# Normalised attention and a leaky-ReLU MLP on one core: the order of products in a half-Strassen batch, a softmax reciprocal one group later, and one multiply moved behind a maximum

## The chip, the core and the metric

The kernel runs on one core of a Trainium2 chip. The metric is the device time in microseconds of one execution. The core has engines that run side by side (in the kernel before, PE was busy for 96% of the span, ACT for 72% and DVE for 67%): TensorE for matmuls (PE in the profile, with PEld for its weight loads), VectorE (DVE), ScalarE (ACT), GpSimd (POOL) and SyncE (SP), which only issues transfers here. The profile lists the instructions of each, and beside a wait the instruction of another engine that ended it. The kernel puts its matmul results into banks of PSUM, and some matmuls have to wait until ACT or DVE has emptied a bank (0.42 us at 355.63, behind ACT's L575; 0.30 us by starts at 361.94, where DVE's L578 ran from 361.26 to 361.88). Idle time of PE in front of a matmul is called a stop here.

The kernel before took 424.06 us in the median of three runs (423.5 to 425.12), and 424.0 us in the median of six once the changed kernel was measured beside it.

## The reference

```python
q, k, v: (8, 12, 448, 64); w_in: (768, 2048); w_out: (2048, 768)
q_n, k_n = rmsnorm(q, g_q), rmsnorm(k, g_k)
scores = q_n @ k_n.T / 8
attn = exp(scores - max); attn = attn / (sum(attn) + 1e-9)
x = (attn @ v) as rows of 768
h = x @ w_in
out = maximum(0.01 * h, h) @ w_out
```

## The kernel before

The attention is cut into 24 units of four heads, three units to a batch. Each unit goes through four groups of score matmuls (L195), one step in the first and two in each other group. Between them PE works off a queue of MLP matmuls of an earlier batch, to keep PE busy. Batches 6 and 7 do part or all of the first MLP product by Strassen's scheme, which makes a product of 2 by 2 blocks from seven block products instead of eight. Batch 6 is the half-Strassen batch: eight plain row blocks ("M", six 448-column matmuls each, L363), and 14 products `(n, s)` of six 224-column matmuls (L565).

The code that the change touches, with cuts marked:

```python
def shift_max(u):                       # the first maximum of a unit, L232, and dg, L234 (DVE)
    ...
def shift_mm(u):                        # L244: dg spread by PE; L245: second maximum; L253: eb (DVE)
    ...
def ex(u):                              # L214: et = exp(scores + eb) (ACT); empties the score slot
    ...
def pv_out(u):                          # L295: P*V copied from PSUM to x32, a single buffer (ACT)
    ...
def zcol_inv(u):                        # L305, L306: 1/sum as Ln and Exp (ACT), then four DMAs to rz
    ...
def xmul_pool(u, eng=nc.gpsimd):        # L321: xt = x32 * rz; on DVE for units 4 to 6
    ...

LATE_HALF = ("M", "M", "M", "M", "M", (1, 2), (2, 2), (7, 2), "M", (6, 2), (1, 3), "M",
             (5, 2), (4, 2), (7, 3), (3, 2), (2, 3), (6, 3), "M", (5, 3), (4, 3), (3, 3))

for u in range(3, NU):                  # NU = 24
    for d in range(4):
        qk(u, STEPS[d])                 # L195
        if d == 0:
            shift_max(u)
            # ... pv_slot(u - 1); zcol(u - 1)
            shift_mm(u)
            pv_out(u - 1)
            zcol_sum(u - 1)
        ex(u)
        # ...
        if d == 0:
            job(zcol_inv, u - 1)
        if d == 1 and narrow(u - 1) and not 5 <= u < 8:
            xmul_pool(u - 1)
        # ... at d == 2: job(prep_rinv, u + 2), then two jobs prep_norm (L167, DVE)
        if d == 2 and 5 <= u < 8:
            job(xmul_sb, u - 1)         # the multiply on DVE
        fill(u, d, jobs)                # queue items, with jobs between them
```

The products of batch 6 share four PSUM banks. A product that starts a new sum needs a bank that an L357 (an M's leaky ReLU), an L575 (a product's leaky ReLU, both ACT) or an L578 or L584 (sums and copies on DVE) has emptied. Of these waits the profile lists 0.30 us for an L357 at 351.00 and 0.42 for an L575 at 355.63.

## Time and profile before

| what | value |
|---|---|
| median of three runs | 424.06 us |
| span of the profiled run | 421.4 us |
| PE busy | 403.2 us, 96% |
| ACT, DVE, POOL busy | 304.5, 282.1, 83.3 us |
| PE busy in 80-100 us | 18.81 of 20 us |
| PE busy in 350-370 us | 18.52 of 20 us |

PE is the engine that sets the time, and its work is the same in both kernels. The table is therefore read for where PE is not busy. The prediction below shows the lines of these places.

### The profile page before, as it was taken

Reading aid. Unit: us, or ns where it says so; the run is one execution under the profiler, and the core shown is the slowest. Engines: PE = TensorE matmul, PEld = TensorE weight load, DVE = VectorE, ACT = ScalarE, POOL = GpSimd, SP = SyncE. Lnnn points to the kernel's source line nnn. Section 1 sums busy time; section 2 is a strip of 40 time slices with the busy share of each in tenths; the row PEclk is TensorE's granted clock in tenths of the full one; section 3 lists DMA queues with packets and bytes.
Section 4 is the critical chain, followed back from the end, with each engine's and each line's share of the span. In section 5 each row is a group of like instructions: output and inputs, shape, how many; then the busy total and the mean of one; then the engine's idle time right before and its main releaser. Section 6 shows DMA issues by size and latency. Waiting matters only on the chain.

```text
span 421.4 us, 9149 instructions
## 1 busy us (share of the span) xinstructions
PE 403.2 (96%) x3731; PEld 217.4 (52%) x3731; DVE 282.1 (67%) x459; ACT 304.5 (72%) x474; POOL 83.3 (20%) x75
## 2 busy tenths in 40 slices
PE   8787999989999999999999999999999999999995
PEld 7454454444445544454445544454445556558953
DVE  5888675888569736576459736467349788547762
ACT  5999877768887689877987689867986666653600
POOL 1967432200010121210220120220110101010000
PEclk9999999999999999999999999999999999999999
DMA  8999996889664995678664796677542470212023
GB/s 273 230 251 258 237 252 91 210 154 199 163 152 75 213 242 98 160 175 176 156 144 78 214 192 139 169 151 186 156 88 45 120 162 2 45 39 75 2 53 98
DMA packets 71949, 62.39 MB, mean 148 GB/s; under 512 B 36324, under 2 KB 67044, under 8 KB 71908
## 3 DMA queue, kind: packets, MB, share of 16 engines
q1 hardware_dynamic: 61312, 49.62, 46.4%
q0 software_dynamic: 10272, 11.80, 18.0%
q8 instruction: 29, 0.48, 0.4%
q10 hardware_dynamic: 324, 0.39, 0.3%
q14 instruction: 12, 0.10, 0.1%
HBM read 45.61 MB, written 11.01 MB: 134 GB/s over the span
## 4 chain that ended last, share of the span: by engine, by line
PE 79%; DVE 9%; ACT 9%; issue 1%; DVEq 0%; ACTq 0%
PE hps L363 25%; PE sT L195 7%; PE sT L341 6%; ACT et L214 5%; PE ma L445 5%; PE md L445 5%; PE mc L445 5%; PE bank L445 5%; PE zc L283 3%; PE op L404 3%; PE bank L565 3%; PE mb L445 3%; DVE n L167 2%; PE warm L743 2%; PE sT L445 2%
## 5 line engine op out<-in xcount | busy, mean ns | idle before, releaser
L214 ACT ACTIVATE et<-sT,eb 128x896 f16<-128x896 f32 x166 | 159.6, 1010 | 17.8 <-PE sT L195 16.1
L363 PE MATMUL hps<-xt,win 128*128 128x448 f16 x594 | 119.9, 353 | 0.4 <-DVE xt L350 0.2
L363 PEld LDWEIGHTS <-win 128*128 128x128 f16 x612 | 56.6, 98 | 59.1 <-issue 10.8
L321 POOL TENSOR_TENSOR xt<-x,rz 128x896 f16<-128x896 f32 x16 | 33.7, 2104 | 145.8 <-DMA rz<-zs 122.7
L167 DVE TENSOR_TENSOR n<-rq,rinv 128x896 f16<-128x896 f32 (+2 forms) x25 | 26.7, 1070 | 52.5 <-ACT rinv L161 49.7
L195 PE MATMUL sT<-qkT 64*64 64x448 f16 x664 | 52.2, 363 | 4.3 <-ACT et L214 3.2
L357 ACT ACTIVATE gt<-hps 128x448 f16<-128x448 f32 x99 | 51.9, 548 | 5.5 <-PE hps L363 5.3
L155 DVE TENSOR_REDUCE ssq<-sq 128x14 f32<-128x896 f32 (+2 forms) x49 | 50.3, 1057 | 0.7 <-ACT sq L144 0.7
L445 PEld LDWEIGHTS <-sa 128*128 128x128 f16 x352 | 32.8, 98 | 26.3 <-issue 6.1
L295 ACT COPY x<-sT 128x896 f32<-128x896 f32 x19 | 17.2, 907 | 37.1 <-DVE sT L245 37.1
L124 POOL DMA_DIRECT2D vt<-in_v_dram x24 | 18.2, 757 | 115.6 <-PE sT L341 108.1
L445 PEld LDWEIGHTS <-gt 128*128 128x128 f16 x264 | 25.2, 98 | 18.7 <-issue 2.1
L195 PEld LDWEIGHTS <-qkT 64*64 64x64 f16 x672 | 15.4, 104 | 37.6 <-issue 32.8
L341 PE MATMUL sT<-et,vt 64*64 64x448 f16 x532 | 28.5, 349 | 0.3
L404 PE MATMUL op<-wout,gt 128*128 128x384 f16 x160 | 28.4, 327 | 0.0
L232 DVE TENSOR_REDUCE sT<-sT 128x1 f32<-128x896 f32 x22 | 24.1, 1094 | 4.7 <-PE sT L195 4.5
L341 PEld LDWEIGHTS <-vt 64*64 64x64 f16 x672 | 20.7, 107 | 11.3 <-issue 1.7
L167 DVE TENSOR_TENSOR n<-rk,rinv 128x896 f16<-128x896 f32 (+2 forms) x26 | 26.1, 1010 | 0.0
L404 PEld LDWEIGHTS <-gt 128*128 128x128 f16 x192 | 17.6, 98 | 14.6 <-issue 3.1
L445 PE MATMUL ma<-wout,gt 128*128 128x384 f16 x128 | 23.5, 326 | 0.0
L426 DVE TENSOR_TENSOR sa<-gt 128x512 f16<-128x512 f16 (+1 forms) x15 | 8.1, 542 | 16.0 <-ACT gt L357 12.1
L144 ACT ACTIVATE sq<-rq 128x896 f32<-128x896 f32 (+2 forms) x18 | 16.3, 913 | 1.2 <-DMA rq<-in_q_dram 1.2
(136 smaller groups left out, 526.8 us busy)
## 6 DMA issues: line engine op xcount, KB each, us to landing
rq<-in_q_dram SPq DMA_DIRECT2D x24, 448.0 KB, 4.3
rk<-in_k_dram SPq DMA_DIRECT2D x24, 448.0 KB, 5.7
out_dram<-ost SPq DMA_DIRECT2D x52, 192.0 KB, 2.9
rz<-zs SPq DMA_DIRECT2D x76, 112.0 KB, 2.3
vt<-in_v_dram POOLq DMA_DIRECT2D x24, 224.0 KB, 5.5
win<-in_moe_w_in_dram POOLq DMA_DIRECT2D x8, 384.0 KB, 12.7
wout<-in_moe_w_out_dram POOLq DMA_DIRECT2D x2, 1536.0 KB, 27.1
out_dram<-ost SPq DMA_DIRECT2D x4, 96.0 KB, 2.1
```

The source lines that it names most:

```text
L124: nc.gpsimd.dma_start(vts[u % NV].rearrange("p a t d -> p a (t d)"), rows(v, u))
L155: nc.vector.tensor_reduce(buf(u, "ssq")[:, ti, :, c[0]:c[1]], buf(u, f"sq{ti}")[:, :, c[0]:c[1]], axis=AXL.X, op=ALU.add)
L167: nc.vector.tensor_tensor(buf(u, "n16")[:, ti, c[0]:c[1]].rearrange("p s a d -> p a s d"), src[:, :, c[0]:c[1]], buf(u, "rinv")[:, ti, :, ...
L195: nc.tensor.matmul(banks[a][64 * r:64 * r + 64, 0:S].rearrange("p (t x) -> p t x", t=NS), kT(u, r, a, t), qT(u, r, a), start=True, stop=True)
L214: nc.scalar.activation(s["et"][:, t], sT[:, :, 0:S], AF.Exp, bias=s["eb"], scale=1.0)
L232: nc.vector.tensor_reduce(s["spare"][:, 511:512], sT[:, :, 0:S], axis=AXL.XY, op=ALU.max)
L321: eng.tensor_tensor(xts[b][:, g], s["x32"], s["rz"], op=ALU.mult)
L341: nc.tensor.matmul(s["pv"][r][64 * a:64 * a + 64, 0:S], vts[u % NV][64 * r:64 * r + 64, a, t], s["et"][64 * r:64 * r + 64, t, a], start=(t ...
L357: nc.scalar.activation(dst, src, AF.Prelu, bias=0.0, scale=1.0, alpha=0.01)
L363: nc.tensor.matmul(hps[:, 0:S], win16[:, kt // 2, kt % 2, ts(ft, P)], xt[:, kt // 2, kt % 2], start=(kt == 0), stop=(kt == KT - 1))
L404: nc.tensor.matmul(op2[:, 0:HC], gt[:, ft, ds(col(t), P)], wout16[:, ft, ds(HC * half, HC)], start=(ft == 0), stop=(ft == FT - 1))
L445: nc.tensor.matmul(bank[:, 0:HC], a[:, f], b[:, f], start=(first and f == 0), stop=(f == HF - 1), skip_group_check=not first)
```

## The change

The intent is to move three things out of PE's way: the products of batch 6 that ask for a bank too soon, the two activations of unit 22's reciprocal that delay the leaky ReLU of the last product, and the multiply of unit 4 that delays the first maximum of unit 6.

```diff
-    LATE_HALF = ("M", "M", "M", "M", "M", (1, 2), (2, 2), (7, 2), "M", (6, 2), (1, 3), "M", (5, 2), (4, 2), (7, 3), (3, 2), (2, 3),
-                 (6, 3), "M", (5, 3), (4, 3), (3, 3))
+    LATE_HALF = ("M", "M", "M", "M", "M", "M", (1, 2), (7, 2), (2, 2), (6, 2), "M", (1, 3), (5, 2), (4, 2), (7, 3), (3, 2), (6, 3),
+                 (2, 3), (5, 3), (4, 3), "M", (3, 3))
@@ two weight sums hung on other products
-                after[7, 2] = [lambda: win_sum(1, 0, (raws, "rq", 3))]
-                after[6, 2] = [lambda: win_sum(2, 0, (raws, "rk", 3))]
+                after[6, 2] = [lambda: win_sum(1, 0, (raws, "rq", 3))]
+                after[1, 3] = [lambda: win_sum(2, 0, (raws, "rk", 3))]
@@ unit 4's multiply
                         shift_max(u)
+                        if u == 6:
+                            xmul_sb(u - 2)
...
-                if d == 2 and 5 <= u < 8:
+                if d == 2 and 6 <= u < 8:
                     job(xmul_sb, u - 1)
@@ the last reciprocal
-                        job(zcol_inv, u - 1)
+                        if u < NU - 1:
+                            job(zcol_inv, u - 1)
...
-                if d == 1 and narrow(u - 1) and not 5 <= u < 8:
+                if d == 1 and narrow(u - 1) and not 5 <= u < 8 and u < NU - 1:
                     xmul_pool(u - 1)
+                if u == NU - 1:
+                    if d == 1:
+                        job(zcol_inv, u - 1)
+                    if d == 2:
+                        xmul_pool(u - 1)
```

## The prediction

> **What bounds the kernel now.** I read the busy shares, the slices and the chain of waits first, then PE's own waits, then the timeline around each of them, and last the program order of both kernels on each engine.
>
> ```profile
> PE 403.2 (96%) x3731; PEld 217.4 (52%) x3731; DVE 282.1 (67%) x459; ACT 304.5 (72%) x474; POOL 83.3 (20%) x75
> PE   8787999989999999999999999999999999999995
> ```
>
> PE has work nearly all the time, and the change neither adds nor removes a matmul (7461 rows on PE's program in both). So the only thing to win is time in which PE stands still. PE's busy time by stretch shows where: about 10 us are lost in the first 60 us, which the change leaves alone; then 20.0 of 20 almost everywhere, but 18.81 in 80-100, 9.28 of 10 in 350-360 and 9.23 in 360-370. PE's waits, with their start times in the timeline, name these places:
>
> ```profile
> 85.82 0.22 PE L244 MATMUL sT<-dg,onesp 128*128 128x64 f16 x2 [0.97 <-DVE dg L234]
> ...
> 351.00 1.29 PE L363 MATMUL bank<-xt,win 128*128 128x448 f16 x6 [0.30 <-ACT gt L357]
> ...
> 355.63 0.73 PE L565 MATMUL bank<-xt,win 128*128 128x224 f16 x6 [0.42 <-ACT gt L575]
> ...
> 361.94 0.73 PE L565 MATMUL bank<-xt,ws 128*128 128x224 f16 x6
> 362.51 1.14 PE L404 MATMUL bank<-wout,gt 128*128 128x384 f16 x6
> 364.28 0.50 PE L404 MATMUL bank<-wout,gt 128*128 128x384 f16 x2 [0.63 <-ACT gt L575]
> ```
>
> Columns: start, length, instruction, and in brackets the idle time before it and who ended it. Between 85.82 and 351.00 PE shows no wait, so what is won at 85 should come through to the end, unless it is given back close by. The change aims at exactly these stops: unit 4's multiply sits before the one at 85.82, the half-Strassen batch (batch 6) runs from 345.9 to 362.5, and the last reciprocal's two activations lie just before 364.28.
>
> [...] So I count lost time from starts. Six 224-column matmuls take 0.575 us from start to start (360.49 to 361.06). The six before 351.00 began at 349.97 and should have given way at 350.54: 0.46 us are lost, where the bracket says 0.30. Likewise 355.63 lost 0.58 (due at 355.05), 361.94 lost 0.30 (due at 361.64, no bracket), and 364.28 lost 0.79 (six 384-column matmuls at 0.1625 make 0.98 from 362.51). Sum in the batch: 2.13 us. At 85.82: zc began at 84.00 and elsewhere takes 0.78 to the next matmul (98.94 to 99.72), so 1.04 us are lost.
> [...] PE does nothing else in the 0.79 us before 364.28. So only a new order can move these stops.
> [...] beside the POOL multiply at 367.91 the L435 subtraction takes 2.57 us, where its neighbours L429 and L432 of the same size take 0.68 and 0.69.
>
> **Part 1: unit 4's multiply behind unit 6's maximum.** DVE around the stop:
>
> ```profile
> 82.89 1.08 DVE L321 TENSOR_TENSOR xt<-x,rz 128x896 f16<-128x896 f32 x1
> 83.90 0.54 DVE L408 COPY ost<-op 128x384 f32<-128x384 f32 x1
> 84.36 1.08 DVE L232 TENSOR_REDUCE sT<-sT 128x1 f32<-128x896 f32 x1
> 85.48 0.29 DVE L234 TENSOR_TENSOR dg<-ident,sT 128x128 f16<-128x128 f16 x1
> 86.08 0.30 DVE L245 TENSOR_REDUCE sT<-sT 128x1 f32<-128x128 f32 x1 [0.31 <-PE sT L244]
> 86.41 0.91 ACT L295 COPY x<-sT 128x896 f32<-128x896 f32 x1 [4.86 <-DVE sT L245]
> 87.21 1.01 ACT L214 ACTIVATE et<-sT,eb 128x896 f16<-128x896 f32 x1
> ```
>
> The scores were there at 82.74, but the multiply (1.01 to the next start) stands in the way. Afterwards DVE goes: ost copy 82.89, maximum 83.35, dg 84.47, so PE's L244 starts at about 84.81: its stop of 1.04 shrinks to 0.03. But the multiply now lies between dg and L245: it starts at about 84.70, and L245 at 85.71 rather than 86.08. Everything behind it on ACT (copy, et) is 0.37 earlier, not 1.0. PE would be back for the next scores at 87.60, and must wait for the slot that et frees at about 87.9 (before: no wait, 88.57). The next ets start when ACT's two zs activations are over, near 88.47 instead of 89.01, 0.54 earlier. The next group of scores already waits inside in the kernel before (eight matmuls from 90.48 show 0.87 where 0.57 is usual), that is, ACT paces PE there. So of 1.04 I keep 0.54: the rest turns into a wait for et. Part 1: **-0.5 us**. The x32 buffer (one only) is no obstacle: the multiply ends at 85.8, the copy into it starts at 86.05.
>
> **Part 2: the new order of batch 6.** I walked the new program order through, group by group, on the clock of before, with start-to-start costs from its trace: an M item (six 448-column matmuls) 1.13, a product 0.575, scores 0.50 and about 0.09 to switch; first matmul of an M to its L357 1.34, of a product to its DVE op 0.84; L357 and L575 0.44 apart, two ets 1.78.
> The stop at 351.00: an M wanted the bank of the M before, whose L357 stood behind two ets until 350.95. Now that place (from 349.98) takes the bank of an M whose L357 ended at 347.8: no stop. The stop at 355.63: product (2,3) wanted a bank two L575 back. In the new order (6,3) is put before it, and (2,3) comes at 355.19, with its bank free at about 355.1. (3,2) at 354.03 waits for a DVE sum that ends at about 354.01: nearly nothing. So unit 23's scores start at 355.86 instead of 356.87: -1.01, less 0.05 for these close ones. DVE is ready: maximum at 356.57, dg done 357.98, wanted at 358.28.
> In unit 23's first group PE now runs (5,3), (4,3), M, (3,3): the last M comes late, where before (3,3) had to wait 0.30 for a sum behind (5,3). (3,3) starts at 360.63, the L404s at 361.21, and their seventh, which needs (3,3)'s L575, is due at 362.19.
>
> **Part 3: the last reciprocal a group later.** ACT just before the stop:
>
> ```profile
> 360.75 1.01 ACT L214 ACTIVATE et<-sT,eb 128x896 f16<-128x896 f32 x1
> 361.65 0.55 ACT L357 ACTIVATE gt<-bank 128x448 f16<-128x448 f32 x1
> 362.07 0.40 ACT L305 ACTIVATE zs<-zs 128x224 f32<-128x224 f32 x1
> 362.50 0.39 ACT L306 ACTIVATE zs<-zs 128x224 f32<-128x224 f32 x1
> 362.80 0.56 ACT L575 ACTIVATE gt<-v 128x448 f16<-128x448 f32 x1
> 363.26 0.96 ACT L575 ACTIVATE gt<-bank 128x448 f16<-128x448 f32 x2
> ```
>
> ACT has no gap here; the two zs take 0.73 (362.07 to 362.80). Without them (3,3)'s L575 starts 0.74 earlier relative to et, and et itself is 1.01 earlier: 361.95, done at 362.52. The L404 goes on at about 362.56 instead of 364.28: parts 2 and 3 together -1.72, less the 0.05. A stop of some 0.4 stays. The reciprocal then comes after two ets, at about 365.2 to 366.0; from its end to the POOL multiply it took 5.0 us before (362.89 to 367.91), so POOL works from 371 to 373.5. Its readers are the x sums at 380 and the matmuls at 382.5, which move forward by under 3 us: some 4 to 6 us in hand.
>
> **Sum.** -0.5 - 1.67 = **-2.2 us**. 424.06 - 2.2 = **421.9 us**, -0.5%.
>
> **Rivals.** (a) Part 1 gives back everything: the multiply delays L245 and with it et. For it: L245 could start at 85.1 but for the multiply. Against it: even so it starts earlier than now. It would make 422.4. (b) Part 1 brings its full 1.0, if PE was not paced by ACT in the group at 90.48: 421.4. (c) The bank waits of batch 6 only move, since four banks serve the same products: (3,2) and (2,3) are within 0.1 us of their releasers in my walk, and L575 or DVE 0.3 us later than I reckon brings stops of that size at both, so 422.5. (d) The late reciprocal collides: POOL's multiply slows another DVE sum, or the zs delay two ets and PE's slot. In the kernel before it already slows L435 to 2.57 without a PE wait, so this costs nothing, or 0.3 at most. (e) All that is won comes back in batch 7. Against it: PE's only wait after 364.28 is 0.2 at 399.77.
>
> **Range and chances.** All stops aimed at sum to 2.13 + 1.04 = 3.2 us, 0.75%. So over 2% faster is out of reach, and over 2% slower (8.5 us) would need a wait larger than all that is listed. The three runs of before spread 1.6 us, so noise is of the size of the effect: 420.9 to 423.3. Faster 0.01, within 2% 0.98, slower 0.01.
>
> **What would show it.** PE's wait at L244 for dg near 85.8 is gone, and in its place stands a wait of about 0.3 for et before L195; busy time of PE in 350-370 goes from 18.5 to nearly 19.5 of 20; no wait for L357 in the batch; one wait for L575 before L404 of about 0.4 instead of 0.63; L435 near 0.7. I am wrong if PE's L195 or L565 show new waits that sum to over 1 us, or if the matmuls of batch 7 wait for POOL.

## The result, and the profile after

The changed kernel took 422.0 us in the median of six runs (420.8 to 422.87), beside 424.0 us for the kernel before. The ratio is 0.9949, with a 95% interval from 0.9928 to 0.997. Ratios here are the mean time of one kernel's fast runs over that of the other's in the same rounds, so not quite the ratio of the medians quoted. Measured again later on one chip (the ninth experiment, e9, below), the ratio was 0.9931, from 0.9917 to 0.9944.

The page of the changed kernel, its busy shares and PE's slices:

```profile
span 419.0 us, 9148 instructions
...
PE 402.7 (96%) x3731; PEld 217.6 (52%) x3731; DVE 279.5 (67%) x459; ACT 304.6 (73%) x474; POOL 82.9 (20%) x75
...
PE   7787999999999999999999999999999999999995
```

PE's work is the same, and the span is 2.4 us shorter. The slice that showed an 8 near 85 us before shows a 9 now. PE's busy time in 350-370 us rose from 18.52 to 19.77 of 20 us. PE's timeline at the places that the prediction listed, with the idle time and its releaser in brackets:

```profile
85.03 0.22 PE L244 MATMUL sT<-dg,onesp 128*128 128x64 f16 x2
...
90.58 0.38 PE L195 MATMUL sT<-qkT 64*64 64x448 f16 x4 [0.39 <-ACT et L214]
...
360.52 1.14 PE L404 MATMUL bank<-wout,gt 128*128 128x384 f16 x6
361.89 0.50 PE L404 MATMUL bank<-wout,gt 128*128 128x384 f16 x2 [0.23 <-ACT gt L575]
```

The stop at L244 is gone, and so are all stops in batch 6 but the last, which is shorter. A new one stands before the scores at 90.58.

**A ruler for half a microsecond.** The runs of one kernel spread by 1 to 2 us, so the times alone can't place the gain. The traces can. PE's instructions are the same ones in the same units in all kernels here, so the start of a given instruction can be compared. I take L244 of unit 5 (72.28 us before) as zero, since nothing changed ahead of it. What differs there arose in the first 72 us and is taken off all later shifts. Three landmarks follow: L244 of unit 7 (99.72), the scores behind the L404 that stops (364.71), and the last group of matmuls (415.70).

| kernel | shift at unit 5 | unit 7, less that | scores behind L404, less that | last matmuls, less that |
|---|---|---|---|---|
| changed | +0.21 | -0.87 | -2.60 | -2.60 |
| e1 multiply only | +0.10 | -0.87 | -0.87 | -0.86 |
| e2 order only | +0.60 | +0.01 | -1.03 | -1.03 |
| e3 reciprocal only | -0.20 | 0.00 | -0.69 | -0.68 |
| e4 two products swapped | +0.62 | +0.01 | -0.60 | -0.59 |
| e5 unit 5's multiply first | +0.50 | -0.28 | -0.27 | -0.27 |
| e6 multiply after the shift | +0.20 | -0.99 | -2.76 | -2.75 |
| e7 late rows last | -0.08 | -0.86 | -3.01 | -3.01 |
| e8 e6 and e7 | +0.47 | -0.99 | -3.15 | -3.15 |
| e9 changed, again | -0.10 | -0.87 | -2.61 | -2.61 |

Between unit 7 and unit 22 the shift of the changed kernel stays within 0.02 us at all 16 L244s. What is won at 85 us is kept to the end, and nothing of it is given back in batch 7.

**Around unit 6.** The timeline of the changed kernel, cut to DVE and ACT (start, length, instruction):

```profile
83.57 1.08 DVE L232 TENSOR_REDUCE sT<-sT 128x1 f32<-128x896 f32 x1
...
84.69 0.29 DVE L234 TENSOR_TENSOR dg<-ident,sT 128x128 f16<-128x128 f16 x1
84.89 1.08 DVE L321 TENSOR_TENSOR xt<-x,rz 128x896 f16<-128x896 f32 x1
...
85.90 0.29 DVE L245 TENSOR_REDUCE sT<-sT 128x1 f32<-128x128 f32 x1
86.22 0.91 ACT L295 COPY x<-sT 128x896 f32<-128x896 f32 x1 [4.46 <-DVE sT L245]
...
87.03 1.01 ACT L214 ACTIVATE et<-sT,eb 128x896 f16<-128x896 f32 x1
```

This clock runs 0.21 us late against before. With that taken off, L244 comes 1.00 us earlier (85.03 - 0.21 against 85.82) and L245 only 0.39 earlier (85.90 - 0.21 against 86.08), because the multiply lies in between (84.89 to 85.97). PE is 1.00 ahead and ACT 0.39, and PE waits for ACT: 0.39 for an et, in front of the scores at 90.58.

**Batch 6's end.** ACT in the changed kernel, from unit 23's first et to its second group:

```profile
359.05 1.01 ACT L214 ACTIVATE et<-sT,eb 128x896 f16<-128x896 f32 x1
359.95 0.58 ACT L575 ACTIVATE gt<-v 128x448 f16<-128x448 f32 x1
360.42 0.55 ACT L575 ACTIVATE gt<-bank 128x448 f16<-128x448 f32 x1
360.84 0.56 ACT L357 ACTIVATE gt<-bank 128x448 f16<-128x448 f32 x1
361.27 0.56 ACT L575 ACTIVATE gt<-bank 128x448 f16<-128x448 f32 x1
362.75 1.91 ACT L214 ACTIVATE et<-sT,eb 128x896 f16<-128x896 f32 x2 [0.92 <-PE sT L195]
364.55 0.39 ACT L305 ACTIVATE zs<-zs 128x224 f32<-128x224 f32 x1
```

The two zs activations have left the row before the last L575, which starts 2.22 us after et (361.27 - 359.05). Before it was 2.95: the last of the two L575 in the row at 363.26 started about 0.44 later (an estimate from the start-to-start time of two L357 or L575), at 363.70, against et at 360.75. They now run in a gap that ACT has anyway between two groups: in front of the et at 368.35 in the kernel before it stood idle for 1.30, and in front of the same et, at 365.96, in the changed kernel it still does for 0.60.

### The profile page after: what moved, and what is told of

Same layout as the page of the kernel before. It is cut to its first block, busy times and chain, and to the rows that moved or that the text cites. A ratio compares the mean times of both kernels' runs of the same rounds, so it can differ in the third digit from the quotient of the medians.

```text
span 419.0 us, 9148 instructions
## 1 busy us (share of the span) xinstructions
PE 402.7 (96%) x3731; PEld 217.6 (52%) x3731; DVE 279.5 (67%) x459; ACT 304.6 (73%) x474; POOL 82.9 (20%) x75
## 4 chain that ended last, share of the span: by engine, by line
PE 83%; ACT 9%; DVE 6%; issue 1%; DVEq 0%; ACTq 0%
PE hps L363 27%; PE sT L195 8%; PE sT L341 6%; ACT et L214 6%; PE ma L445 5%; PE md L445 5%; PE mc L445 5%; PE bank L445 5%; PE bank L565 4%; PE op L404 3%; PE zc L283 3%; PE mb L445 3%; PE warm L743 2%; PE sT L445 2%; DVE n L167 1%
## 5 line engine op out<-in xcount | busy, mean ns | idle before, releaser
L357 ACT ACTIVATE gt<-hps 128x448 f16<-128x448 f32 x100 | 52.4, 549 | 5.4 <-PE hps L363 5.1
L404 PE MATMUL op<-wout,gt 128*128 128x384 f16 x160 | 28.4, 327 | 0.0
L404 PEld LDWEIGHTS <-gt 128*128 128x128 f16 x192 | 17.6, 98 | 14.0 <-issue 2.9
```

The source lines that it names most:

```text
L357: nc.scalar.activation(dst, src, AF.Prelu, bias=0.0, scale=1.0, alpha=0.01)
L404: nc.tensor.matmul(op2[:, 0:HC], gt[:, ft, ds(col(t), P)], wout16[:, ft, ds(HC * half, HC)], start=(ft == 0), stop=(ft == FT - 1))
```

## The experiments

Nine experiments ran; all were correct. Each is told by its edit against the kernel before (e1 to e5) or against the changed kernel (e6 to e9).

**e1, the multiply alone.** The edit is the part "unit 4's multiply" of the diff above.

> Only unit 4's multiply is moved behind unit 6's maximum; everything else as before. Times of the same landmark (PE's L244 of unit 7, at 99.72 us in the kernel before, and the L404 that stops at 364.28) are compared after taking off the shift that both kernels already show at L244 of unit 5 (72.28). Theory from the trace of the changed kernel: -0.87 us at both, made of -1.00 at L244 of unit 6, +0.12 and +0.29 in the two score groups behind it, and -0.28 at the sixth matmul of the first M of batch 1, which no longer waits for unit 5's multiply. Rival (the prediction's step): -0.54, nothing at that M. Second rival: the three parts interact and the gain appears only with the new order, so nothing is left at 364. The three stops at 351, 355.6 and 364.3 must stay.

It took 423.0 us beside 423.59 us, ratio 0.9981 (0.9969 to 0.9993). Its landmarks are -0.87 at unit 7 and -0.87 behind the L404, and the three stops of batch 6 have the brackets of before (0.30, 0.42, 0.63). So this part is independent of the others and worth 0.87 us, not the 0.54 of the prediction.

**e2, the order alone.** The edit is the first two parts of the diff.

> Only the new order of batch 6 (with the two weight sums hung on other products). Theory: the stops of 0.46 and 0.58 go, the one of 0.30 before (3,3) goes but comes back as part of a longer stop before the seventh L404, because the two zs activations still stand in front of its L575: in all -1.0 us from L244 of unit 22 to L195 behind that L404, and a stop there of about 1.1 us. Rival: the order alone does all of parts 2 and 3, -1.7 us, and the reciprocal's place is worth nothing. Unit 6's stop of 0.97 at L244 must stay.

It took 422.67 us, ratio 0.9975 (0.9965 to 0.9984), landmark -1.03. PE's timeline at the end of batch 6:

```profile
361.79 1.14 PE L404 MATMUL bank<-wout,gt 128*128 128x384 f16 x6
363.85 0.50 PE L404 MATMUL bank<-wout,gt 128*128 128x384 f16 x2 [0.93 <-ACT gt L575]
```

Six L404s take 0.98 us from start to start, so the seventh was due at 362.77, and 1.08 us are lost here, where the kernel before lost 0.79. The 0.30 in front of (3,3) has only moved behind it. The order alone wins 1.03, and the rival (1.7) falls. The new order and the two moved weight sums were not run apart, and of the stops that went only the one at 355.63 was tried alone (e4).

**e3, the reciprocal alone.** The edit is the last part of the diff.

> Only the last softmax reciprocal and its multiply a group later, old order. Theory: -0.73 us, the two zs activations (start of the first to start of the next L575), all of it at the L404 that stops at 364.28, whose bracket falls to nothing; the stops at 351.0, 355.63 and 361.94 stay. Rival: ACT's work is only moved, the two ets behind it come 0.8 later and PE waits for them, net 0. Second rival: the late multiply on POOL holds up batch 7 (a wait on POOL or on rz before L565).

Its landmark is -0.69, all of it at the L404, which now runs without a bracket (the line shows all eight as one row):

```profile
362.32 1.57 PE L404 MATMUL bank<-wout,gt 128*128 128x384 f16 x8
```

The row of 1.57 is still 0.11 longer than the 1.46 that eight L404s take in e7, so about 0.1 of the stop is left without a bracket. The other stops stay, and no wait for POOL appears. The ratio is 0.9987 (0.9978 to 0.9996), at 423.23 us in the median of 20. One of the 20 executions took 1408.55 us; it is counted as slow and left out of the ratio (the median of the other 19 is 423.07). I have no explanation, and no other kernel here had such a run. The sum of the three parts done alone, 0.87 + 1.03 + 0.69 = 2.59, is the 2.60 of the whole change: they add, and no interaction shows.

**e4, two products swapped.** This asks whether the stop at 355.63 is a matter of one bank.

```diff
-                 ... (3, 2), (2, 3),
-                 (6, 3), "M", (5, 3), (4, 3), (3, 3))
+                 ... (3, 2), (6, 3),
+                 (2, 3), "M", (5, 3), (4, 3), (3, 3))
```

> Old kernel, with two neighbouring products of batch 6 changed over: (6,3) before (2,3). Theory (a bank that two L575 must free first): the stop of 0.58 at 355.63 shrinks to 0.1 or less, -0.5 us there, all else the same, so 351.0, 361.94 and 364.28 keep their stops. Rival (ACT is simply behind, any product would wait): the stop moves to the next product and nothing is won.

The landmark is -0.60. PE's timeline at the two products:

```profile
355.08 0.74 PE L565 MATMUL bank<-xt,ws 128*128 128x224 f16 x6
355.65 0.74 PE L565 MATMUL bank<-xs,ws 128*128 128x224 f16 x6
356.23 0.73 PE L565 MATMUL bank<-xt,win 128*128 128x224 f16 x6
```

The starts are 0.575 us apart, so the whole 0.58 is gone and comes back nowhere. Only (2,3) had to wait, for its bank, and one product in between gives the two L575 ahead enough time. The single look (one run, not compared in rounds) took 423.2 us.

**e5, unit 5's multiply before the norms.** The trace of the changed kernel showed a gain that the prediction does not have. The first M of batch 1 in the kernel before, and the multiply on DVE that writes its last third:

```profile
95.80 1.58 PE L363 MATMUL hps<-xt,win 128*128 128x448 f16 x6
```

```profile
95.70 1.08 DVE L321 TENSOR_TENSOR xt<-x,rz 128x896 f16<-128x896 f32 x1
```

Six such matmuls take 1.30 elsewhere. The first four need units 3 and 4, the last two need unit 5, whose multiply ends at 96.78. No wait is listed: the row of 1.58 has no bracket. The experiment moves only this multiply, in the kernel before:

```diff
                         job(prep_rinv, u + 2)
+                        if u == 6:
+                            job(xmul_sb, u - 1)
                         ... # two jobs prep_norm
-                if d == 2 and 5 <= u < 8:
+                if d == 2 and u in (5, 7):
                     job(xmul_sb, u - 1)
```

> Old kernel; only unit 5's multiply on DVE is put before the two norms of unit 8 instead of behind them. Theory (a stop that the waits do not list: the first M of batch 1 needs unit 5's product for its last two matmuls): that M's six matmuls take 1.30 instead of 1.58 and all behind it comes 0.28 us earlier, while the stop of 0.97 at unit 6's L244 stays. Rival (the 0.28 is a matmul or weight-load irregularity and has nothing to do with the multiply): no change at the M. The norms and the transposing DMA come 1 us later; if that matters, unit 8's scores wait.

```profile
86.32 0.22 PE L244 MATMUL sT<-dg,onesp 128*128 128x64 f16 x2 [0.97 <-DVE dg L234]
...
96.30 1.30 PE L363 MATMUL hps<-xt,win 128*128 128x448 f16 x6
```

The M takes 1.30, the landmark is -0.28, and the stop at L244 stays. So the hidden stop was real, and unit 5's multiply was its cause. In the changed kernel the same multiply starts 1.00 us earlier (94.91, less the shift of 0.21, against 95.70) and comes in time. The single look took 423.39 us, which does not show a gain of this size.

**e6, the multiply behind the second maximum too.** In the changed kernel the multiply holds L245 back. Here it goes behind L245 and L253. As x32 is a single buffer, the copy into it must wait for the multiply, so et goes ahead of the copy.

```diff
                         shift_max(u)
-                        if u == 6:
-                            xmul_sb(u - 2)
...
                             shift_mm(u)
+                            if u == 6:
+                                xmul_sb(u - 2)
+                                ex(u)
                             pv_out(u - 1)
...
-                    ex(u)
+                    if (u, d) != (6, 0):
+                        ex(u)
```

> Changed kernel, with unit 4's multiply put behind the second maximum and the shift (L245, L253) too, and, since its buffer x32 is single, unit 6's first et put before the copy into x32 on ACT. Theory (between dg and L245 the multiply holds L245 back 0.6 us, and with it et and the next two score groups, which stand 0.12 and 0.52 us): L245 comes at about 0.26 us behind L244 instead of 0.87, the stop of 0.39 in front of L195 in unit 6's third group falls to 0.15 or less, and from the next unit on all is about 0.4 us earlier than in the changed kernel. Rival (ACT's total work in these groups sets the pace, not when it begins): 0.1 us or nothing.

Its landmarks are 0.12 ahead of the changed kernel at unit 7 and 0.16 ahead behind the L404, less than half of what I expected. The single look took 420.66 us. ACT in this kernel, and below it the multiply on DVE:

```profile
85.86 1.01 ACT L214 ACTIVATE et<-sT,eb 128x896 f16<-128x896 f32 x1 [4.12 <-DVE eb L253]
86.97 0.91 ACT L295 COPY x<-sT 128x896 f32<-128x896 f32 x1
87.77 0.39 ACT L305 ACTIVATE zs<-zs 128x224 f32<-128x224 f32 x1
...
88.49 1.89 ACT L214 ACTIVATE et<-sT,eb 128x896 f16<-128x896 f32 x2
```

```profile
85.79 1.09 DVE L321 TENSOR_TENSOR xt<-x,rz 128x896 f16<-128x896 f32 x1
```

ACT starts 0.36 earlier than in the changed kernel (85.86 against 86.22), but the next two ets start only 0.15 earlier (88.49 against 88.64). The other 0.21 is lost in front of the copy: it starts 1.11 after et, where ACT's next instruction starts 0.90 after this et in the changed kernel (87.93 against 87.03). The copy has to wait for the multiply, which DVE runs from 85.79 to 86.88; from the copy on, the row takes as long as it did. The stop before the third group is 0.37 instead of 0.39, since PE itself is 0.12 earlier there. So the result has the size that the rival named, but it does not show the rival's reason. ACT did begin 0.36 earlier, the single buffer took 0.21 of it, and 0.12 of the rest reached PE by unit 7. A second buffer for x32 would have told more, but this kernel does not build with one: the build stops with the message that the last pool asks for 12 KB per partition, and that 9.78 are left. That stays open.

**e7, late rows last.** The seventh L404 waits for the rows that (3,3) writes. The other half of gt is ready earlier, so the sum can begin there. The edit reorders every L404 product of this pair of batches; the stop is at the first.

```diff
-        for ft in range(8 * part, 8 * part + 8):
+        order = list(range(8 * part, 8 * part + 8))
+        if pair == 3:
+            order = [[8, 9, 10, 12, 13, 14, 15, 11], list(range(8))][part]
+        for i, ft in enumerate(order):
             nc.tensor.matmul(...,
-                             start=(ft == 0), stop=(ft == FT - 1))
+                             start=(part == 0 and i == 0), stop=(part == 1 and i == 7))
```

> Changed kernel, with the first L404 product of batch 6 and 7's pair summed in another order: the half of gt that is ready first comes first, its youngest row last. Theory (what is left of the stop, 0.39 us from its due time, is only the wait for the L575 of product (3,3)): the stop is gone, -0.39 us at the next scores, and nothing else moves. Rival: the stop moves to the row written by the last L357, or the sum waits for the bank, and under 0.2 us is won.

```profile
360.23 1.46 PE L407 MATMUL bank<-wout,gt 128*128 128x384 f16 x8
361.62 0.57 PE L195 MATMUL sT<-qkT 64*64 64x448 f16 x8
```

(L407 is L404 of the others.) All eight run without a stop, and the landmark is 0.41 ahead of the changed kernel's. The single look took 420.12 us.

**e8 and e9, both together and the changed kernel again.** They ran on one chip with five rounds each. e8 has the edits of e6 and e7; e9 is the changed kernel.

> Changed kernel with the edits of the sixth and seventh experiment together. Theory: they lie 270 us apart and add, -0.15 and -0.41 us at the same landmarks as there, so -0.57 against the changed kernel and about -3.2 against the kernel before (ratio about 0.9925), all of it still there at the last matmul. Rival: the second gain shrinks because units in between take up the first; or the time does not follow the landmarks because the tail or the start differs.

> The changed kernel unaltered, on the same chip and in the same rounds as the eighth experiment, so that the two can be compared. Theory: ratio to the kernel before 0.994 (-2.6 us), 0.5 us above the eighth. Landmarks as in its first trace: -0.87 us at L244 of unit 7 and -2.60 at L195 behind the seventh L404, both against the kernel before and less the shift at L244 of unit 5. Rival: the ratio 0.9949 of the first measurement (-2.2 us) was right and the landmarks overstate.

e8 took 420.36 us (419.86 to 421.19), ratio 0.9925 (0.9912 to 0.9937). e9 took 420.49 us (420.44 to 421.42), ratio 0.9931 (0.9917 to 0.9944). The kernel before took 423.54 us. By the landmarks e8 is 0.54 us ahead of e9 (-3.15 against -2.61), near the 0.16 + 0.41 = 0.57 of the parts. By the clock they can't be told apart, since the intervals overlap, and the two profiled spans are both 418.7 us. For the two profiled runs the first column of the table says why: e8 had lost 0.57 us against e9 by unit 5 (+0.47 against -0.10), ahead of all edits. So e8 is the best version that I have by its PE timeline, and not shown faster than the changed kernel by its times.

**What goes with the spread.** The windows view of 10 to 20 us in the kernel before and in e2 (time of PE, PEld, DVE, ACT and POOL, then the granted TensorE clock):

```profile
10.00:20.00 10.00, 7.53 (x102) 5.07 (x99) 8.36 (x16) 9.62 (x15) 9.39 (x13) 1.00 1.07 231
```

```profile
10.00:20.00 10.00, 9.18 (x97) 5.87 (x93) 7.94 (x14) 9.06 (x14) 9.42 (x13) 0.66 0.99 206
```

In four of the eleven profiles (e2, e4, e5, e8) this clock is 0.66, and these four have the late starts, +0.47 to +0.62 at unit 5. With the clock at 1.00 (the changed kernel, e1, e6, e7, e9) the shift lies between -0.10 and +0.21. e3 is between in clock, 0.83, but not late, -0.20. Of the six timed runs of the changed kernel, the one with a mean clock of 1.000 was the fastest (420.8), and the five with 0.990 to 0.996 took 421.52 to 422.87. The 32 executions of the kernel before in the rounds of e1 to e3 say the same: the median is 423.93 for the 13 with a mean clock of 0.990 to 0.992, 423.67 for the 7 with 0.994 to 0.996 and 423.37 for the 12 with 0.998. The place fits too. Unit 0's spread of dg (L250, the counterpart of L244) starts at 11.74 in e2 and 11.78 before, unit 1's at 20.40 against 19.54, so e2 falls behind in the stretch in which its clock is low. This goes together in the runs and was not tested by an experiment, and what lowers the clock was not shown. For differences under 0.5 us it means that a time alone does not settle them.

## Why the prediction was right

**The total.** Predicted 421.9 us and -2.2 us. Measured 422.0 us, with a ratio that makes -2.2 us of 424.0 in the first measurement and -2.9 us of 423.54 (0.0069) in e9. The landmarks say -2.60. The prediction's steps make 0.4 less than that, so it is partly luck that the first median lies within 0.1 us of the forecast: the interval of its ratio reaches from -1.3 to -3.1 us.

**Lost time counted from starts.** The step that takes stops from start to start held. e4 won 0.60, where this count has 0.58 and the bracket 0.42. In the kernel before, a stop of 0.46 us by starts showed as 0.30, one of 0.58 as 0.42, one of 0.79 as 0.63: each bracket is 0.16 less. This is what the listed length of the row before exceeds its time from start to start by (0.74 against 0.575, 1.14 against 0.98). At L244 that is 0.85 against 0.78, and 1.04 showed as 0.97. The stop of 0.28 inside the row of six at 95.80 showed as none, so the lengths of like rows have to be compared too (1.58 against 1.30).

**Part 1.** Predicted -0.54, measured -0.87 (e1). The multiply does lie between dg and L245, L244's stop did shrink to nothing (1.00 of 1.04), and L245 came 0.39 earlier, where 0.37 was reckoned. Two terms were off. The step "PE would be back for the next scores at 87.60, and must wait for the slot that et frees at about 87.9" was wrong in its slot. The changed kernel's first four scores start at 87.78, while et runs until 88.04. (The time itself held: 87.78 less the shift is 87.57, and the prediction's own 84.81 plus the 2.75 from L244 to these scores before makes 87.56, not 87.60.) Only the second four waited, and the cost is 0.12. The pacing by ACT in the next group is there as said, with 0.39 in its bracket, and costs 0.29 more. The two ets came 0.58 earlier (88.64 less 0.21, against 89.01), where 0.54 was reckoned. So -1.00 + 0.12 + 0.29 = -0.59, near the 0.54. The other 0.28 is a step that the prediction lacks: "Between 85.82 and 351.00 PE shows no wait" was read as "loses no time". The stop inside the row of six matmuls at 95.80 has no bracket, and e5 shows that it was there and what it was (1.58 us before, 1.30 in e5).

**Parts 2 and 3.** Predicted -1.72 less 0.05 for two close places, measured -1.73 (2.60 - 0.87). Part 2 alone gave -1.03 and part 3 alone -0.69; the walk had -1.01 for the batch, and 0.74 for the two zs. The 0.05 was not needed: (3,2) and (2,3) start 0.575 after their forerunners. The walk held step by step: on the clock of before (+0.66 here), unit 23's first et starts at 359.71 and the L575 of (3,3) at 361.93, where 359.74 and 361.95 were reckoned. The stop that was to stay, "some 0.4", is 0.39 by starts (361.89 against 361.50 due). As a sign it was put beside the 0.63 of a bracket, which mixes the two counts: the bracket fell to 0.23.

**The rivals.** (a) and (c) did not come true. (b), the full 1.0 of part 1, is nearest in its sum, but not for its reason: ACT did pace PE in the group at 90.48, and another stop made up for it. For (d), the late multiply on POOL, the L435 subtraction took 0.68 instead of 2.57 and POOL's multiply 2.08 instead of 2.51; L435 is over at 366.69, and the multiply starts at 369.78, so the two no longer meet. For (e), the last matmuls have the same shift as the scores at 364.

## What to carry to other kernels

When one engine is busy 96% of the time, list each of its stops from start to start, walk the program order of the change past them with measured costs, and ask of every stop removed which engine holds the next one: here 1.00 us won at one matmul was worth 0.59 two groups later. Compare the lengths of like rows of matmuls too: the row of six at 95.80 took 1.58 us where its like took 1.30, and held a stop of 0.28 that no list of waits shows. For gains under the spread of the runs, compare the start of the same instruction in two traces, less the shift at one ahead of the change.
